# A mixed attention and MLP kernel: its written-out job order replaced by another, with the first four input tiles at the head of the DMA queue

## The chip, the cores and the metric

The kernel runs on one core of one Trainium2 chip. The time is device microseconds of one launch; lower is better. Three runs of the kernel before were timed: 707.80, 707.37 and 707.33 us, median 707.37 us. One further execution was taken by the hardware profiler; all rows quoted below come from it.

## The reference

For 2048 tokens of width 512 the reference computes `x + attention(xn) + mlp(xn)` with `xn = layernorm(x)`.

```
xn = layernorm(x)
# attention: 32 heads of width 16, the tokens in 4 segments of 512
q, k, v = xn @ wq, xn @ wk, xn @ wv
for s in range(4):                       # segments, in order
    a_dot = softmax(qs @ ks.T * scale + causal mask) @ vs
    a_mem = phi(qs) @ M / (phi(qs) @ z + 1e-6)
    o = g * a_mem + (1 - g) * a_dot
    M += phi(ks).T @ vs;  z += phi(ks).sum()
out_A = o @ wo
# mlp, per token
out_B = gelu(layernorm(xn) @ w1 + b1) @ w2 + b2        # 512 -> 1792 -> 512
return x + out_A + out_B
```

## The kernel before

**Number format.** Every large product is computed from float16 pairs: a value is split into a high and a low float16 half, and three products (high-high, high-low, low-high) are added in PSUM. The weights are scaled by powers of two that depend on their norms, so each weight must be loaded whole, squared and summed (`w_square`, ScalarE), turned into a scale (`w_scale`, a few tiny TensorE products and small ops), and split (`w_split`) before it can be used.

**Units.** The attention is cut into 16 units `i` (segment `i // 4`, group `i % 4` of 8 heads). A unit goes through these jobs:

- `T` or `T2`: the projections to queries and keys (TensorE, lines 497 or 528); the result is split into high and low halves, written to DRAM (`kd`, `qd`) and read back in another layout (`kst`, `qst`), all by the SP queue (lines 567 to 569 and 577).
- `M` (12 per unit): logits in PSUM (line 684) of which VectorE takes row maxima into `mc` (line 691). `R`: the maxima are transposed, written to DRAM (`md`) and read back as two more rows of `qst` (lines 704 and 707).
- `S` (12 per unit): logits again, transposed (line 724), then the exponential on ScalarE (line 729) into `pt` and the causal select on GpSimd (line 738).
- `pv`, `PV` (two times four): `pt` times values (line 753); `O` (three parts): division by the softmax sum; `Z`, `Qd`, `Q`: the memory part; `N`, `K`: the update of the memory.

**MLP.** It is cut into 16 half steps `j`: `D`/`D2` (products with w1, lines 497 and 528), `G` (seven Gelus on ScalarE with two table loads, lines 844 and 975), `H` (the split of the hidden values: GpSimd, ScalarE, GpSimd, lines 851 to 853), `e` (14 jobs of six products with w2, line 878). `V`/`V2` make values, `o2`/`out` the output projection, `X`/`Xt` the normalised input (loads at line 461, statistics at 407 to 422, transposes at 483 and 516), `ratio` a row of factors, `A` the accumulator loads.

**The loads.** `wl` issues weight loads on the SP queue: `qk` (the first column block of wk and wq, line 269), `QK` (the other three), `v`, `1a`/`1b` (the halves of w1, line 294), `2a`/`2b` (w2, line 297), `o`. `hold` is one small VectorE memset on the second block of wk. `wm` is `w_square`, `wf` is `w_scale`, `ws` is `w_split`.

**Fillers.** `warm` (14 jobs, line 922) are eight products of a tile of ones each whose result nobody reads.

**The order.** `streams()` makes lists of jobs; each list keeps its own order. The string `ORDER` merges them: each letter names a list, and the next job of that list is issued. The letters that matter here are: a input, c weight loads, C to J the preparation of the weight parts qk, QK, v, 1a, 2a, 1b, 2b, o, e constants, f and g the first segment's keys and queries, i `M` and `R`, j `S`, k `pv`, l `O`, m memory, n `V`, o `D`, p `G` and `H`, q `e`, r `out`, s `A`, t `warm`, u to z and A, B the paired jobs (`T2`, `V2`, `o2`, `D2`) in two phases. Since every engine takes its instructions in the order in which they are issued, this string is the order of TensorE, VectorE, ScalarE, GpSimd and of the SP queue's DMA issues alike.

```
bank = iter("".join(BANKS))
def dense():
    return dps.tile([P, 512], F32, name="ps" + next(bank), bufs=1)
...
todo = [iter(st) for st in streams()]
for c in "".join(ORDER):
    key = next(todo[NAMES.index(c)])
```

`BANKS` gives, for each PSUM tile that is asked for, which of the eight banks it takes. A job whose bank still holds a result that VectorE or ScalarE has not read yet waits on TensorE, and everything behind it.

Of the kernel before, what the change touches and what calls it, by code (L numbers as in the profile page):

```python
# [56 lines left out]
def streams():  # L57
# [59 lines left out]


ORDER = (
    "ecCcaacccCcaDDaaccDcDtCttttatDcaDctaatcCCtEeeDtEcbdfEtFFFDFGcFGFFgcEFEGFhDFoGfoFsoooEoiGotiDHcHGGHiicHcGEgHiGGE"  # L120
    "pHnIpniinioHiitiiHIDpHnIDIomciiooHhiqiqiqqDpjpqijqjqsijjioIijkHkHkkijsmIijqiqjqjiasqjjaIIfooIIipkkkkgplhAqpBAql"
    "jjBAljjqBpqijiqjqqiisIpkkkIkmiqjqiqijiqjqjqiqjjsfgsiiqqAJiqBJpikkkktaplphAlABBijApsijBjjijiqijqaaqippqqiqiqalak"
    "kmkkiqaqjqqjiqaqjqbaAjiBippmuijjvkkkkjApAjpBjlBlqhqjqqjqijqqiilkakkkjiqqJijqiqJqjjiqqjAiijBikpkkkJiiulwJJiJlmvl"
    "xymjjzwjjjxiAjikpskkkppiiBiyiijzjiqsjqjqjiqsiqjikmkkkphlqimulimvqAqjBjqlqjqjqjqjAammkkkkqjBijAjismjBjiAjiiBippk"
    "kkklAhipslBuimipvqqqqqqpiaqAqiqqiqqlmqiqBiApiBjApijiBijAjiBspjjiiaapkakkkmijijqjqhajajqqsiiqjqaakpmkkksillubmvq"
    "jqqqjqjqjqjAjqklkmkkmmjjBAjjiBjiwjikiikkpklxiiulhimlivAyBpqqiizipppqwiiqixiiqijqjqjjqjiqiqjiiskmkkksjiqqijqjqjA"
    "jisjBiypmhkkkkmpjpszjjllujmjvAAjBpmkkmlkkApBjBqqjqiqiqjqiqijqqjjiqqiqiaipmskkkpkhqqAiiBqipplqqsiupqliqmvqqsmlAj"
    "qqBjAqjqaAqBqqBiAiAspiappBijBAijjBaakaikkpkpiqijqjqiqjjqqqajjiqqqiipakkkkmiqaqaplqbqmlujmjvpAjjBjAhjBlkmkkkmjqp"
    "AjmiBjqijqqpjiqijqikkkklqiluimvwixiqiiqqqliqAiqqBpiiyjiijjzjjwijixiipksmkkksmjjyijjijzijspkkkkliAluimvqBpmqAqjB"
    "jAjqjmBpjqjqqiislkkkkiqjiqijqjqijiqjiqjqiikkppkklpAiilBuimvAqBpljqqjqjjqpAjqjBmkkkkiqjiqjqiqjjiqjqijqqiAsiBsipi"  # L130
    "ppkkikikpAAslpAiBilsBBqmqqqpqjplqqjqjqjqqjqjmkkpmkkjqqjqjjqqjjkkppkklllqqqqqqqqqqqrrrr"
)

BANKS = (
    "012345670234571265073241563702415637024156307241567302461730524612730546172305461732054732054270354270325743074"
    "250753402754302730542730542730574327430253026517425612574612547612457621462517642517642517651304276153042763105"
    "371640251367245024675024675024675204657206547123067123540623540635715274016534016534160534163045136401536145023"
    "767650231476502310231654371650271650247310247103246571247615023402736470326740327406320632327342067342067306175"  # L140
    "342107642710654327154327106543651027651027431043104365271065423765432714036510342765314027653102476351026351026"
    "365310265310261021602160251630164703164275167452031674013640137640512640512643705370512371237123075172513072512"
    "350172350172315701253706142671042536742536714025314530202671425367014730673140617430614370614376102576104376107"
    "610410341764103257641254103245176521470635214063756340765340765340765340765340762153765321453201475601473265010"
    "615302631053216302516302630251026531026531654702316503126035124607350746351027463510265310625317254063176317402"
    "540217521754021754021547012501427501472501245763012453012763012415276415276527641257641526741572461547263015264"
    "730156473232013256473256473256473256041736041736"
)


# [854 lines left out]
```

## Time and profile before

| | |
|---|---|
| median of three timed runs | 707.37 us (707.33 to 707.80) |
| the profiled execution's own time | 702.23 us |
| its span, first to last instruction | 700.5 us |
| TensorE busy | 681.1 us (97%), 8111 products |
| VectorE busy | 535.3 us (76%) |
| ScalarE busy | 522.9 us (75%) |
| GpSimd busy | 349.8 us (50%) |
| mean granted TensorE clock | 0.995 |

The span leaves out 1.7 us of the profiled execution around it. The timed runs are about 5.1 us longer than the profiled one. Rows of the profile name the engine (PE is TensorE, PEld its weight load, DVE VectorE, ACT ScalarE, POOL GpSimd, SPq the SP queue's issues), the line of the kernel, the operation and the tiles, written tile first. A busy TensorE is not a TensorE at its peak: the ends of products are modelled and overlap, so the time from one job's first product to the next job's is the better measure.

### The profile page before, as it was taken

The numbers are of one execution on the slowest core, as the hardware profiler recorded it, in microseconds if no ns is written. First come the engines' busy times: TensorE is split into PE (matmuls) and PEld (weight loads), VectorE is DVE, ScalarE is ACT, GpSimd is POOL, SyncE is SP. The second block draws the span as 40 slices with busy tenths as digits, with TensorE's granted clock in tenths as the row PEclk, the third lists the DMA queues.
The fourth block names the chain that finished last, engine by engine and source line by source line (L and its number), as shares of the span: only waits on it lengthen the run. The fifth ranks groups of instructions, "written<-read, shape, count | busy, mean of one in ns | idle before, by whom it ended". The sixth has DMA issues, their size and how long they took to land.

```text
span 700.5 us, 20441 instructions
## 1 busy us (share of the span) xinstructions
PE 681.1 (97%) x8111; PEld 421.1 (60%) x8111; DVE 535.3 (76%) x1695; ACT 522.9 (75%) x1013; POOL 349.8 (50%) x533
## 2 busy tenths in 40 slices
PE   8799999999999999999999999999999999999997
PEld 6464566575554577575566656577664656556533
DVE  4499877788588678899688847979778786969542
ACT  6989897778777668768883896677983667877970
POOL 5376667364524435646425355546462155464652
PEclk9899999999999999999999999999999999999999
DMA  9965222330402224022404224132031223131101
GB/s 283 264 188 185 65 62 63 76 78 18 124 3 82 67 72 104 29 68 62 107 3 122 46 50 137 17 109 47 5 92 47 78 76 94 17 103 37 19 1 60
DMA packets 51803, 55.33 MB, mean 79 GB/s; under 512 B 4782, under 2 KB 40636, under 8 KB 51708
## 3 DMA queue, kind: packets, MB, share of 16 engines
q1 hardware_dynamic: 49404, 49.84, 24.5%
q0 software_dynamic: 2304, 4.20, 3.6%
q8 instruction: 63, 1.03, 0.6%
q14 instruction: 32, 0.26, 0.1%
HBM read 36.99 MB, written 17.04 MB: 77 GB/s over the span
## 4 chain that ended last, share of the span: by engine, by line
PE 53%; ACT 15%; DMA 11%; DVE 9%; POOL 6%; issue 4%; SPq 2%; DVEq 0%; ACTq 0%; POOLq 0%
PE ps L528 20%; PE ps L878 12%; PE ps L753 8%; ACT pt L729 7%; PE ps L684 4%; DMA qd<-hl 3%; PE ps L724 3%; DMA qst<-qd 3%; DVE ps L691 2%; PE ps L497 2%; ACT hT L852 2%; PE ps L896 1%; ACT hT L844 1%; DVE hl L566 1%; POOL hT L853 1%
## 5 line engine op out<-in xcount | busy, mean ns | idle before, releaser
L691 DVE CUSTOM_DVE_ANT_0 ps<-ps,mask 128x512 f32<-128x512 f32 (+3 forms) x512 | 235.1, 521 | 26.2 <-PE ps L684 21.1
L729 ACT ACTIVATE pt<-ps,qkcs 128x512 f32<-128x512 f32 (+1 forms) x384 | 206.1, 627 | 30.3 <-PE ps L724 25.6
L878 PE MATMUL ps<-w2s,hT 64*128 64x512 f16 x1344 | 180.4, 376 | 0.6 <-ACT nD L762 0.3
L738 POOL TENSOR_SCALAR_AFFINE_SELECT pt<-pt 128x256 f32<-128x256 f32 x256 | 100.4, 424 | 104.0 <-ACT pt L729 103.3
L528 PE MATMUL ps<-xnT,w1s 64*128 64x256 f16 x2352 | 147.4, 269 | 0.4 <-ACT pt L729 0.3
L528 PEld LDWEIGHTS <-w1s 64*128 64x128 f16 x2352 | 121.8, 94 | 19.3 <-issue 1.6
L878 PEld LDWEIGHTS <-hT 64*128 64x128 f16 x1344 | 78.9, 94 | 52.2 <-issue 3.9
L853 POOL TENSOR_TENSOR hT<-hh,hT 128x512 f16<-128x512 f32 x64 | 67.1, 1049 | 76.9 <-ACT hT L852 76.9
L724 PE MATMUL ps<-qst,kst 50*128 50x256 f16 (+3 forms) x512 | 81.2, 296 | 2.6 <-DMA qst<-md 0.8
L684 PE MATMUL ps<-kst,qst 48*128 48x512 f16 (+3 forms) x512 | 77.8, 297 | 3.0 <-DVE mc L691 1.0
L753 PE MATMUL ps<-pt,vt 128*32 128x512 f32 (+3 forms) x1024 | 79.4, 436 | 0.5 <-POOL pt L738 0.5
L691 DVE DVE_READ_ACCUMULATOR2_ANT mc<- 128x1 f32 x512 | 71.2, 139 | 0.1
L528 PE MATMUL ps<-xnT,wqs 64*128 64x512 f16 x288 | 66.0, 376 | 0.0
L528 PE MATMUL ps<-xnT,wks 64*128 64x512 f16 x288 | 66.0, 376 | 0.0
L852 ACT ACTIVATE hT<-hh 128x512 f16<-128x512 f32 x64 | 36.8, 575 | 34.5 <-POOL hh L851 34.4
L825 DVE SCALAR_TENSOR_TENSOR hT<-ps,sc,sr 128x256 f32<-128x256 f32 x112 | 48.9, 476 | 14.1 <-PE ps L528 11.7
L753 PEld LDWEIGHTS ps<-pt,vt 128*32 128x32 f32 x1024 | 32.1, 109 | 42.0 <-issue 28.6
L851 POOL TENSOR_SCALAR hh<-hT,sc 128x512 f32<-128x512 f32 x64 | 42.4, 662 | 18.5 <-ACT hT L844 16.4
L684 PEld LDWEIGHTS <-qst 48*128 48x128 f16 x512 | 31.7, 94 | 28.8 <-issue 11.6
L724 PEld LDWEIGHTS <-kst 50*128 50x128 f16 x512 | 34.4, 94 | 24.0 <-issue 8.6
L844 ACT ACTIVATE hT<-hT,b1t 128x256 f32<-128x256 f32 x112 | 46.9, 496 | 1.7 <-DVE hT L825 1.5
L783 POOL TENSOR_TENSOR nN<-nN,oT 128x512 f32<-128x512 f32 x16 | 20.3, 1268 | 43.3 <-DVE oT L597 43.3
(227 smaller groups left out, 1021.5 us busy)
## 6 DMA issues: line engine op xcount, KB each, us to landing
kd<-hl SPq DMA_DIRECT2D x48, 128.0 KB
kst<-kd SPq DMA_DIRECT2D x32, 192.0 KB
qd<-hl SPq DMA_DIRECT2D x48, 128.0 KB
qst<-qd SPq DMA_DIRECT2D x32, 192.0 KB
acc<-in_A_x_dram SPq DMA_DIRECT2D x16, 256.0 KB
acc<-in_B_b_dram POOLq DMA_DIRECT2D x16, 256.0 KB, 4.0
out_dram<-acc SPq DMA_DIRECT2D x16, 256.0 KB
xt<-in_A_x_dram SPq DMA_DIRECT2D x14, 256.0 KB
```

The lines of the kernel that those rows point to most:

```text
L528: w = T.matmul(ps[a], lhs(a, k, u)[r], rhs(a, k, v)[r], start=ph == 0 and k == 0 and m == 0, stop=ph == 1 and k == n - 1 and m == 2, skip_ ...
L684: T.matmul(p[:, o:o + n], stk[i, 0][r, t, P * qb:P * qb + P], stk[i, 1][r, t, :n], start=True, stop=True)
L691: V.tensor_tensor_reduce(p[:, o:o + n], p[:, o:o + n], mask[:, 512 - n:], 1.0, -3e38, OP.add, OP.max, mc[:, 16 * b + 4 * t + qb:16 * b + 4 ...
L724: T.matmul(p[:, o:o + n], stk[i, 1][r, t, P * kb:P * kb + P], stk[i, 0][r, t, P * kb:], start=True, stop=True)
L729: A.activation(e[:, OFF[kbs[0]]:OFF[kbs[0]] + o], p[:, :o], AF.Exp, scale=qkcs[:, 1, i % NG:i % NG + 1])
L738: G.affine_select(v, v, pattern=[[0, 2], [1, P]], compare_op=OP.is_ge, fill=0.0, base=0, channel_multiplier=-1)
L753: T.matmul(p[32 * c:32 * c + 32, P * kb:], vt[s, kb][:, 4 * g + c, 16 * odd:16 * odd + 32], pt[i, 2 * c + odd][:, OFF[kb]:OFF[kb] + LEN[kb ...
L825: V.scalar_tensor_tensor(hzs[fh][:, fi, :], p[:, :256], col(F1 + fh), srow[hs][:, 256 * hh:256 * hh + 256], op0=OP.mult, op1=OP.mult)
L844: A.activation(z, z, AF.Gelu_apprx_tanh, bias=b1t[:, FH * (j % 2) + f:FH * (j % 2) + f + 1])
L852: A.activation(hT[:, z, 0, :], t, AF.Copy)
L853: G.tensor_tensor(hT[:, z, 1, :], t, hT[:, z, 0, :], op=OP.subtract)
L878: w = T.matmul(pes[j][a], hTs[fh][r, fi, u, P * a:P * a + P], w2s[r, fo, v, :], start=n == 0 and m == 0, stop=fi == FH - 1 and m == 2, ski ...
```

## The change

`ORDER` and `BANKS` are replaced by other strings of the same length (1307 letters, 1158 digits). Each letter occurs as often as before, so the same jobs are issued and each list keeps its own order; what changes is how the lists are merged, and which bank each PSUM tile takes.

```diff
 ORDER = (
-    "ecCcaacccCcaDDaaccDcDtCttttatDcaDctaatcCCtEeeDtEcbdfEtFFFDFGcFGFFgcEFEGFhDFoGfoFsoooEoiGotiDHcHGGHiicHcGEgHiGGE"
-    "pHnIpniinioHiitiiHIDpHnIDIomciiooHhiqiqiqqDpjpqijqjqsijjioIijkHkHkkijsmIijqiqjqjiasqjjaIIfooIIipkkkkgplhAqpBAql"
...
-    "ppkkikikpAAslpAiBilsBBqmqqqpqjplqqjqjqjqqjqjmkkpmkkjqqjqjjqqjjkkppkklllqqqqqqqqqqqrrrr"
+    "eettaccaCtCcDDcactCaDacDCcDDceccttttaatacaCDEtEbDttccDfdFFFDaFEGFFccEGFsgEDFoGFEFgchFEfoooHoGHGiGHHiioGGsoHppnc"
+    "iiiniiGGniiHHIHniiHooDImiqhiqiipIooiIDpqjqpscijqqjijiqiHIjqqijEHqiIImkkkkoIsjiqjsojjiqHjjafIoiIqkkpkkgplApqABIj"
...
+    "sspppkkkplsAiiBABiABqqppplqqjjqjljmqjqjqmqpmkkkkqqjqjqjqjqjqqjppkkkkqqqqqqqqlqqlqqlrrrr"
 )
 BANKS = (
-    "012345670234571265073241563702415637024156307241567302461730524612730546172305461732054732054270354270325743074"
+    "012345670123567403142573610425731642057316424057316402576314025763140257631402631402631402630124603126402631460"
...
```

Read out, the SP queue's issues begin, before, with wk and wq block 0, then the four tiles of the first 512 tokens, then `QK` (three), `v` (two), the two small loads, `1a`, `2a`. After, they begin with two input tiles, wk and wq block 0, the other two input tiles, then `QK`, `v`, the small loads, `1a`, `2a` as before; the loads `X(1,0,0)` of the next segment follow the first projection's write-out, where before they came some 130 jobs later. The fillers stand, before, at places 21 to 53, 89, 125 and 289 of the order; after, at places 2 to 50, 349 and 602 (twelve of them ahead of the first projection, against ten before). In both, the first projection `T(0,0,1)` is followed on TensorE by the scale of `1a` before the second projection `T(0,0,0)`; before, the scale of `v` and a filler stand between the two as well.

More of the change, by code (lines that the diff above doesn't have):

```diff
@@ L119 @@
 ORDER = (
-    "ecCcaacccCcaDDaaccDcDtCttttatDcaDctaatcCCtEeeDtEcbdfEtFFFDFGcFGFFgcEFEGFhDFoGfoFsoooEoiGotiDHcHGGHiicHcGEgHiGGE"
-    "pHnIpniinioHiitiiHIDpHnIDIomciiooHhiqiqiqqDpjpqijqjqsijjioIijkHkHkkijsmIijqiqjqjiasqjjaIIfooIIipkkkkgplhAqpBAql"
-    "jjBAljjqBpqijiqjqqiisIpkkkIkmiqjqiqijiqjqjqiqjjsfgsiiqqAJiqBJpikkkktaplphAlABBijApsijBjjijiqijqaaqippqqiqiqalak"
-    "kmkkiqaqjqqjiqaqjqbaAjiBippmuijjvkkkkjApAjpBjlBlqhqjqqjqijqqiilkakkkjiqqJijqiqJqjjiqqjAiijBikpkkkJiiulwJJiJlmvl"
-    "xymjjzwjjjxiAjikpskkkppiiBiyiijzjiqsjqjqjiqsiqjikmkkkphlqimulimvqAqjBjqlqjqjqjqjAammkkkkqjBijAjismjBjiAjiiBippk"
@@ L125 @@
[L125 to L129, printed above, removed]
@@ L130 @@
-    "jAjqjmBpjqjqqiislkkkkiqjiqijqjqijiqjiqjqiikkppkklpAiilBuimvAqBpljqqjqjjqpAjqjBmkkkkiqjiqjqiqjjiqjqijqqiAsiBsipi"
-    "ppkkikikpAAslpAiBilsBBqmqqqpqjplqqjqjqjqqjqjmkkpmkkjqqjqjjqqjjkkppkklllqqqqqqqqqqqrrrr"
+    "eettaccaCtCcDDcactCaDacDCcDDceccttttaatacaCDEtEbDttccDfdFFFDaFEGFFccEGFsgEDFoGFEFgchFEfoooHoGHGiGHHiioGGsoHppnc"
+    "iiiniiGGniiHHIHniiHooDImiqhiqiipIooiIDpqjqpscijqqjijiqiHIjqqijEHqiIImkkkkoIsjiqjsojjiqHjjafIoiIqkkpkkgplApqABIj"
+    "pAjlBjjBjqhpqqjilkikJkkiIaiqqjiqjqjjqiqjiqqijcfgqiiqAiqiBkkkpkipAlmJpBAlhiBijApjiBisjqjqijqaqaqpsjqiiqialiqpsak"
@@ new lines @@
+    "kkkmpaqqqjqiqjqitjaAabBiJpjuijjvJkkkmkpjAqjqqjplqBjAqlBjjqqiiqilJkkkkiqijqjqiqjiqjjqAiaJhjBiiJkkkkplAiuiBiJmvwj"
+    "mjxlwjjjlaxyiijzipsikpkkkpiiyjjizjjqqijqiqijqismkkkkplimshlqquimvqqqjAalqjBjjqqjjqAmkkkkjsiBjAjijBiAjjiBiismkkp"
+    "mpkklspilAuhBimipvqpqiqqqqqAqiqiqqmqqiqBiiAiBpitplijApijBjjiAjijBaskiapkkkimajjqqhqaijajqjqqjiaakikkkplmqlsbumj"
+    "vjqqqjqqjqjAjlqmkkkkjBjmjihimjAijiBjiikkkkpilipwiulimvplmAxpyiiBziwiisxiiqqijpqjqiqijqjqjiqiqqjikkkkmsasjiqjqqi"
+    "jqjAihjBjypkkkkmjpzjjsllumjjvAApBjBlpmkkkmkAqBjpqmqjiqiqjqqjiqijqiqjppsAiiqqiBhqqipkkkklqppqqiiuiqlsqimvqqAjqqq"
@@ L132 @@
+    "qqjajBqAlmABqBiAiApapiBjBpjiAiijBasakkkpkpaiqijqqjiqijjqjqqajpiqqiskkkkamqiaqapqqlhbqumljjmjvAjpAjBjlBkkkmkjAjj"
+    "BjmijqiqqjiqipipkkkklmuiliqqmqvqiqqwiqiixiqqiqAiiBilpyjijzijpwjjjxiiskipmskkkjjyijmsjijzjikkkkpliquqlimvAqmlqjB"
+    "AjBjAjqmjBjqisipkkkksiqijqijqjqjiqijqijqiqpipkkkklpAiiBluimvAqBpljqqjqjqjApjqjBmkkkkqijqijqqjiqjijqiqjqiAiBiiki"
+    "sspppkkkplsAiiBABiABqqppplqqjjqjljmqjqjqmqpmkkkkqqjqjqjqjqjqqjppkkkkqqqqqqqqlqlqqlrrrr"
 )
 BANKS = (
-    "012345670234571265073241563702415637024156307241567302461730524612730546172305461732054732054270354270325743074"
@@ L138 @@
[L138 to L147, printed above, removed]
+    "012345670123567403142573610425731642057316424057316402576314025763140257631402631402631402630124603126402631460"
@@ new lines @@
+    "321406321640321362401362401362574062406214305672305762057632057623057360253765302765302531402765312405312756340"
+    "763517264107421607412607412607410276347516302476023514670514670542632632170632170632170631273106237106237150465"
+    "074162350741354162354135074162074162354351620743516207417642013756471536453716453716471647157315764315726405674"
+    "321054302156743145637021456370237140237145637563756021437561450234576513746052173452317460521746035217465246521"
+    "476154276152746161746174561274120374516325071463205762305761243057612437643760152015243760143760512431205142310"
@@ new lines @@
+    "452310452310453214053210457362457362140562174305630567472413056724156742174567241576254715471546271305461305130"
+    "513134613460513274605270513274601535346012753461026134601263041263041263041263047512637512675306740617245306145"
+    "732046517326513726513751375126372637263571260471263504325604756132756132705461273054670354637504162375047504203"
+    "475342750275032475032754023702543750423570354270163540163270163563427563427342756347254763245762345736240157243"
+    "601574321574603215743215743215743215743261057261"
```

## The prediction

> **What bounds the kernel now.** First the page's totals, then who TensorE waits for, then single stretches.
>
> ```profile
> span 700.5 us, 20441 instructions
> ...
> PE 681.1 (97%) x8111; PEld 421.1 (60%) x8111; DVE 535.3 (76%) x1695; ACT 522.9 (75%) x1013; POOL 349.8 (50%) x533
> ```
>
> TensorE has work for all but 19.4 us. The order neither removes nor adds a product, so it can gain only from those 19.4 us, from slow products, and from ends that the busy time covers. In the view of waits (time, times, longest) the named part is small:
>
> ```profile
> PE ps L360 <- ACT w1s L328: 3.8, 2, 2.6
> ...
> PE ps L684 <- DVE mc L691: 1.0, 2, 0.8
> PE ps L684 <- DMA qst<-qd: 0.9, 2, 0.5
> ```
>
> The largest is the start. In the timeline (start, length, idle time before):
>
> ```profile
> 0.82 0.44 SPq L269 DMA_DIRECT2D wks<-in_A_wk_dram  x1
> ...
> 1.86 0.97 SPq L461 DMA_DIRECT2D xt<-in_A_x_dram  x2
> ...
> 5.74 0.69 DVE L407 BATCH_NORM_STATS2 st<-xt 128x6 f32<-128x512 f32 x1 [4.76 <-DMA xt<-in_A_x_dram]
> ...
> 11.50 5.52 SPq L294 DMA_DIRECT2D w1s<-in_B_w_dram  x4
> ...
> 18.68 2.76 PE L497 MATMUL ps<-xnT,wks 128*128 128x512 f16 x12
> ...
> 23.45 1.70 ACT L328 ACTIVATE w1s<-w1s 128x1792 bf16<-128x1792 f32 x1 [0.40 <-DMA w1s<-in_B_w_dram]
> ...
> 27.11 0.59 PE L360 MATMUL ps<-am,ones 128*128 128x1 f32 x2 [1.23 <-ACT w1s L328]
> ...
> 27.98 4.36 PE L497 MATMUL ps<-xnT,wqs 128*128 128x512 f16 x12
> ```
>
> The reader sees three clocks of the start. The input tiles let VectorE begin at 5.74 us; the first projection `T(0,0,1)` runs at 18.68; the second, `T(0,0,0)`, stands behind the scale of w1's first half, which waits for w1 to land (23.4 us) and for ScalarE's squares, until 27.1. The table by stretches (length, busy time of each engine, granted clock) shows the rest:
>
> ```profile
> 24.00:25.00 1.00, 0.00 (x0) 0.00 (x0) 0.72 (x3) 1.00 (x1) 0.00 (x0) 0.72 1.05 389
> ...
> 30.00:31.00 1.00, 1.00 (x4) 0.38 (x3) 0.00 (x0) 1.00 (x4) 0.07 (x1) 0.50 0.21 70
> 31.00:32.00 1.00, 1.00 (x6) 0.40 (x5) 0.00 (x0) 1.00 (x1) 1.00 (x1) 0.86 0.00 0
> ...
> 60.00:70.00 10.00, 9.19 (x97) 5.23 (x94) 8.47 (x32) 9.14 (x17) 7.02 (x9) 1.00 0.37 93
> ...
> 650.00:660.00 10.00, 9.97 (x133) 6.09 (x133) 7.94 (x21) 9.87 (x18) 6.35 (x7) 1.00 0.10 19
> 660.00:670.00 10.00, 9.91 (x91) 4.41 (x88) 2.46 (x4) 9.89 (x19) 7.10 (x12) 1.00 0.08 15
> ```
>
> From 24.4 us (clock 0.72 as a mean of one stretch) to 31.3 us the granted clock is 0.50, so the twelve products of `T(0,0,0)` take 4.36 us where the same twelve took 2.76 at 18.68. From 28 to 650 us TensorE is nearly full. From 650 to 676 us ScalarE is the full engine.
>
> **The change part by part.**
>
> *The head of the DMA queue.* Ahead of w1's first half both orders load the same: 0.5 MB of first blocks, 1 MB of input, 1.5 MB of `QK`, 1 MB of `v`, 1.8 MB of w1. Two input tiles pass 0.5 MB of weights; the other two stay behind the same 1 MB of neighbours. VectorE can begin on the first two perhaps 2 us sooner, but the joint statistics need all four tiles, which end at the same byte. `T(0,0,1)` gains about 1 us (an estimate: two of four 0.69 us statistics done early). That gain then meets the wait at 23.45 us: w1 lands behind the same bytes, ScalarE squares it for the same 3.6 us, TensorE still has the scale of `1a` ahead of `T(0,0,0)`. So both kernels stand at about 28 us with the same projections done. Value 0. Bounds: the best is that the half clock is gone when `T(0,0,0)` begins, 4.36 − 2.76 = −1.6; the worst that it lasts for a second stretch of 6.9 us (24.4 to 31.3), in which a full TensorE does half its work, +3.4. The input tiles `X(1,0,0)` now pass two parts of `1b` in the queue; `1b`'s scale keeps its place in the order (job 106 in both), with more `D` and `T` products ahead of it: 0.
>
> *The fillers.* Of 14, eleven stood before 28 us, and three behind, where TensorE has other work:
>
> ```profile
> 45.49 1.04 PE L922 MATMUL ps<-ones 128*128 128x256 f16 x8
> ...
> 61.89 0.99 PE L684 MATMUL ps<-kst,qst 48*128 48x256 f16 x4
> 62.99 1.03 PE L922 MATMUL ps<-ones 128*128 128x256 f16 x8
> 63.96 0.50 PE L684 MATMUL ps<-kst,qst 48*128 48x384 f16 x6
> 64.87 1.46 PE L497 MATMUL ps<-wvs,xnT 128*128 128x512 f16 x6 [0.41 <-DVE mc L691]
> ```
>
> After, two stand behind 28 us. One filler less is −1.0 (bounds: 0, if a wait takes its place, and −1.0).
>
> *The first unit's maxima.* The same fence shows a cluster: from 61.89 to 62.99 four products of `M` take 1.10 us, and from 63.96 to 64.87 six take 0.91, where VectorE is the late one. At full pace the pairs take about 0.43 each time (a pair of 512 columns side by side is 0.22). That is 1.1 us lost. After, `V(0,1)`, `V(0,2)` and `V(0,3)`, each 2.6 us of TensorE work (half of it is the 1.46 row), stand between the pairs `M 3 to 5`, `6, 7`, `8, 9`, `10, 11`. Value −1.1; bounds 0 (VectorE had other work here, 8.47 of 10 us) and −1.1.
>
> *The round trip from projection to first maxima.* `M(i,0)` needs `kst` and `qst`, which go through DRAM. I counted the TensorE work that the order puts between a unit's projection and its `M(i,0)`, with these rows: a job `e` is 0.65 us (two in 1.46 with the end), a pair of `D2` phases 2.6, the four `pv` 2.4.
>
> ```profile
> 660.96 1.46 PE L878 MATMUL ps<-w2s,hT 64*128 64x512 f16 x12
> ...
> 517.16 1.47 PE L528 MATMUL ps<-xnT,w1s 64*128 64x256 f16 x24
> ...
> 192.77 2.36 PE L753 MATMUL ps<-pt,vt 128*32 128x512 f32 x32
> ```
>
> Before, from unit 2 on, three units have 12.1 us or less (2, 4 and 12), and the view of waits gives 0.9 us to this cause. After, six have (2, 6, 8, 12, 13, 14, the least 11.4: unit 8 lost an `e`, a `D2` phase and two `S` from its cover). Three more at 0.9 / 3 is +0.9. Bounds: 0 (a filled bank hides it) and +1.5 (0.5 each, the longest).
>
> *Clusters of `M` and `S`.* Each hands TensorE's bank to VectorE or ScalarE for longer than it took to fill:
>
> ```profile
> L691 DVE CUSTOM_DVE_ANT_0 ps<-ps,mask 128x512 f32<-128x512 f32 x128 | 86.9, 717 | 13.9 <-PE ps L684 13.0 <-PE ps L724 0.4
> ...
> 552.01 0.52 PE L724 MATMUL ps<-qst,kst 50*128 50x512 f16 x2
> 552.23 0.41 PE L684 MATMUL ps<-kst,qst 48*128 48x256 f16 x2
> 552.85 0.62 PE L684 MATMUL ps<-kst,qst 48*128 48x512 f16 x2 [0.20 <-DVE mc L691]
> 553.28 0.87 PE L724 MATMUL ps<-qst,kst 50*128 50x384 f16 x6
> ```
>
> Here five in a row hold TensorE from 552.01 to 553.97, 2.0 us for about 0.9 us of products: 1.1 lost. Over the trace I find a loss of 0.04 us for a lone `M` or `S`, 0.18 for two in a row, 0.22 for three, 0.77 for four and five. Before there are 140, 80, 19 and 6 such rows, after 131, 95, 18 and 2: 28.1 us against 27.9 us. Value −0.2. Bounds ±3: −3 if the four long rows that go take their loss with them, +3 if the fifteen new pairs cost as much as the dearest do.
>
> *The end.* ScalarE is full here, in one chain:
>
> ```profile
> 654.13 3.04 ACT L844 ACTIVATE hT<-hT,b1t 128x256 f32<-128x256 f32 x7
> ...
> 670.02 6.20 ACT L729 ACTIVATE pt<-ps,qkcs 128x512 f32<-128x512 f32 x12
> ...
> 677.41 0.63 ACT L852 ACTIVATE hT<-hh 128x512 f16<-128x512 f32 x1 [1.19 <-POOL hh L851]
> ```
>
> The last Gelus need the last `D2`; behind them both orders have 28 jobs `e`, unit 15's `S`, `pv` and `O`, and four `out`, and between the last Gelus and the last exponential ScalarE has the same jobs. The new order spreads `e` more evenly among the `S`; that moves TensorE's waits, not ScalarE's end. ScalarE is idle for 0.24 us from 650 to 670. Value −0.2; bounds −0.3 and +0.7 (one `e` too late).
>
> *Sum.* 0 − 1.0 − 1.1 + 0.9 − 0.2 − 0.2 = −1.6 us: span 698.9, the profiled execution's own 702.23 us becomes 700.6, and the median of the runs, which lies 5.1 us higher and moves with it, 707.37 − 1.6 = **705.8 us**, 0.23% faster.
>
> One rule of the Trainium skill bears on the start (TensorE: Matmul & The Clock Gate, Part 1: The HAM clock gate): the clock goes to half after a free-running window of about 3.4 us without work and comes back after one busy window. The trace agrees as far as it goes: 0.50 from 24.4 us, back at 31.3, 3.3 us into `T(0,0,0)`. The new order has no product between `T(0,0,1)`, its small transpose and the `1a` scale, so by the rule the half clock comes for certain, but leaves 3.4 us after 28 us at the latest, 1.7 us lost against the 1.6 lost now. By the page, rival C below would need a further idle window and is less likely than I make it.
>
> **The rivals.**
>
> A, the forecast: small gains near 60 us, a little back in round trips: 705.8 us. For it: each term has a row. Against it: four of five terms are near the size of a single wait.
>
> B, the middle gets tighter than counting shows. Rows of two and more `M` and `S` cost 23 us (28.1 less 140 × 0.04). If the new banks and neighbours take a quarter, it is −5.8 more: 700.0 us. For it: 0.04 against 0.18 us shows how much a neighbour matters. Against it: there are as many such rows as before, 245 and 246, and VectorE and ScalarE have the same work.
>
> C, slower: the half clock lasts for a second stretch, to about 38 us. Place: between `T(0,0,1)` and the `1a` scale, where the filler and the scale of `v` no longer stand. It decides if TensorE, after 28 us, has to wait again for the splits of w1 (ScalarE is full there, 1.00 at 30 us), so that the clock isn't given back. Price +3.4: 705.8 + 3.4 = 709.2 us. Against it: at 30 us TensorE is busy 1.00 even now.
>
> D, nothing: the waits only change places. w1's landing holds the start and ScalarE the end, and what is saved near 60 us is lost at the next `M`: 707.2 us.
>
> **How the numbers follow.** A difference of 0.2%, 1.4 us, is about what a measurement of this kernel can tell from none. Chances: A 0.40, B 0.25, C 0.18, D 0.17. A's own range is 703.5 to 707; just over half of it lies beyond 1.4 us. Faster: 0.24 of A, all of B and 0.01 of D, 0.50. Same: 0.15 of A and 0.13 of D, 0.28. Slower: 0.18 of C, 0.01 of A and 0.03 of D, 0.22. The range takes B with it and reaches past C: 699.5 to 710.
>
> **What would show it.** Right: w1's squares begin at 23 to 24 us and `T(0,0,0)` at 27.5 to 28.5; two fillers behind 28 us; 60 to 70 us with TensorE over 9.7 of 10; three to six round-trip waits of 0.3 to 0.5 us; from the last Gelus to the end within 0.7 us of now (46.4 us from 654.1). Wrong: `T(0,0,0)` ahead of 26 us, which would mean that w1 landed early and the queue's head mattered; a stretch at half clock behind 32 us (C); busy time of TensorE moving by over 3 us between 100 and 650 us (B, or its reverse).

## The result and the profile after

Timed against the kernel before, the changed kernel is faster: a median of 699.12 us against 705.31, ratio 0.992 with an interval of 0.9896 to 0.9943. In a second, later timing it was 698.12 against 703.91, ratio 0.9928 (0.9902 to 0.9955). So the change brings 5 to 6 us. The forecast was 1.6 us. Its sign was right, its size was not.

The profiled execution took 698.73 us, 3.5 us less than the 702.23 of before.

First the page of after, the lines that answer to those of before:

```profile
span 697.0 us, 20435 instructions
...
PE 677.4 (97%) x8111; PEld 432.8 (62%) x8111; DVE 533.4 (77%) x1695; ACT 523.4 (75%) x1013; POOL 351.2 (50%) x533
```

The products are the same 8111. TensorE's busy time is 3.7 us shorter and its idle time the same (19.6 us against 19.4). Its waits (time, times, longest), though, are not fewer:

```profile
PE ps L360 <- ACT w1s L328: 5.0, 2, 3.6
PE ps L684 <- DMA qst<-qd: 2.7, 7, 0.6
PE ps L724 <- ACT pt L729: 1.8, 4, 0.8
...
PE ps L483 <- POOL xt L430: 1.3, 1, 1.3
```

The wait at the start went from 3.8 to 5.0 us, that for the projection's round trip from 0.9 to 2.7. All the waits that the view lists came to 13.1 us and come to 14.2. By these rows alone one would expect a slower kernel. The timeline of the start, after:

```profile
19.16 2.75 PE L497 MATMUL ps<-xnT,wks 128*128 128x512 f16 x12
...
23.80 1.70 ACT L328 ACTIVATE w1s<-w1s 128x1792 bf16<-128x1792 f32 x1 [0.17 <-DMA w1s<-in_B_w_dram]
...
27.46 0.59 PE L360 MATMUL ps<-am,ones 128*128 128x1 f32 x2 [1.44 <-ACT w1s L328]
...
28.34 0.99 PE L360 MATMUL ps<-am,ones 128*128 128x1 f32 x4
29.19 5.17 PE L497 MATMUL ps<-xnT,wqs 128*128 128x512 f16 x12
```

`T(0,0,0)` begins 1.2 us later than before and takes 0.8 us longer. The scale of `v` (line 360, x4) now stands just ahead of it, at half clock, and takes 0.99 us. (The section on the change names it between the two projections for the kernel before alone; it stands there in both, but behind the scale of `1a` now.) Before, it stood in an idle place:

```profile
21.28 0.50 PE L360 MATMUL ps<-am,ones 128*128 128x1 f32 x4
```

The table by stretches (length, busy PE, PEld, DVE, ACT, POOL, then the granted clock, DMA share and GB/s):

```profile
27.00:28.00 1.00, 0.54 (x3) 0.54 (x3) 0.00 (x0) 0.97 (x5) 0.00 (x0) 0.65 1.17 298
...
33.00:34.00 1.00, 1.00 (x4) 0.44 (x3) 1.00 (x2) 1.00 (x2) 1.00 (x2) 0.50 1.05 283
34.00:35.00 1.00, 1.00 (x10) 0.72 (x8) 0.95 (x1) 1.00 (x3) 0.41 (x1) 0.94 1.16 183
...
60.00:70.00 10.00, 10.00 (x111) 5.64 (x111) 9.82 (x39) 7.51 (x17) 7.41 (x8) 1.00 0.39 97
```

The half clock now lasts from 27.3 us (0.65 as the mean of that stretch) to 34.1 (0.94), where before it lasted from 24.4 to 31.3. In the second profile of the changed kernel, which comes below, it lasts from 24.7 to 35.0. At 60 to 70 us TensorE is full, where it had 9.19 of 10. The maxima of the first unit now have values (`V`) between them:

```profile
61.34 0.50 PE L684 MATMUL ps<-kst,qst 48*128 48x256 f16 x4
61.77 2.76 PE L497 MATMUL ps<-wvs,xnT 128*128 128x512 f16 x12
64.47 0.50 PE L684 MATMUL ps<-kst,qst 48*128 48x384 f16 x6
```

The four products have 0.43 us until the next job begins, and so have the six (to 64.90 us), where they had 1.10 and 0.91 before. And the end, from the last Gelus:

```profile
650.76 2.90 ACT L844 ACTIVATE hT<-hT,b1t 128x256 f32<-128x256 f32 x7
```

From 650.76 to the span's end at 697.0 are 46.2 us; before it was 46.4.

**A curve that finds the place.** The order of jobs differs, so rows can't be set side by side. I gave each TensorE job the median of its kind's time in the trace of before, and read off when each kernel has done the same amount of that work. Fillers count as no work, so one that is taken out shows as a gain. Each column is in us, against the first profile of the kernel before, whose time stands at the left; the kernels are described below.

| time in before | after | after, 2nd | before, 2nd | `abb` | `baa` | `aba` | `rt_cover` | `best` |
|---|---|---|---|---|---|---|---|---|
| 30 | +1.6 | +1.5 | +0.8 | +1.3 | +1.1 | +1.2 | +2.3 | +2.3 |
| 56 | +1.3 | +1.3 | +1.3 | +3.7 | +0.9 | +1.3 | +2.2 | +3.1 |
| 65 | −1.4 | −1.4 | +0.8 | +1.0 | +0.9 | −1.4 | −0.5 | +0.4 |
| 87 | −2.1 | −2.2 | +0.7 | +0.3 | +0.9 | −2.1 | −1.3 | +0.3 |
| 215 | −4.1 | −4.4 | +2.4 | −1.1 | +1.6 | −4.1 | −3.4 | −2.0 |
| 255 | −4.1 | −4.6 | +2.5 | −1.0 | +1.5 | −3.9 | −3.4 | −1.8 |
| 360 | 0.0 | −0.4 | +2.4 | +0.1 | +5.4 | −2.8 | +5.8 | −1.9 |
| 402 | −1.9 | −2.3 | +2.5 | +0.1 | +3.9 | −2.8 | +3.8 | −1.8 |
| 567 | −2.8 | −3.6 | +3.9 | −0.7 | +2.6 | −3.9 | +3.0 | −2.6 |
| end | −3.5 | −4.1 | +4.0 | −0.7 | +2.0 | −4.5 | +3.0 | −3.2 |

Before's fillers behind 28 us stand at 45.5, 63.0 and 140.4 us, after's at 164.2 and 306.3. The reader should see three things: a gain of 3.4 us from 56 to 87 us, another of 2.0 to 215 us, and a loss of 4.1 us from 255 to 360 us (1.0 of it a filler), of which about half comes back at once.

### The profile page after: what moved, and what is told of

It reads as the page before. It is cut to its first block, busy times and chain, and to the rows that moved or that the text cites. A ratio compares the mean times of both kernels' runs of the same rounds, so it can differ in the third digit from the quotient of the medians.

```text
span 697.0 us, 20435 instructions
## 1 busy us (share of the span) xinstructions
PE 677.4 (97%) x8111; PEld 432.8 (62%) x8111; DVE 533.4 (77%) x1695; ACT 523.4 (75%) x1013; POOL 351.2 (50%) x533
## 4 chain that ended last, share of the span: by engine, by line
PE 63%; ACT 13%; DMA 10%; DVE 6%; POOL 4%; issue 3%; SPq 1%; ACTq 0%; DVEq 0%; POOLq 0%
PE ps L528 25%; PE ps L878 14%; PE ps L753 7%; PE ps L684 5%; ACT pt L729 4%; DMA qd<-hl 4%; DMA qst<-qd 4%; PE ps L497 3%; PE ps L724 3%; DVE ps L691 2%; ACT hT L844 2%; PE ps L896 2%; POOL hT L853 1%; ACT hT L852 1%; DMA w1s<-in_B_w_dram 1%
## 5 line engine op out<-in xcount | busy, mean ns | idle before, releaser
L729 ACT ACTIVATE pt<-ps,qkcs 128x512 f32<-128x512 f32 (+1 forms) x384 | 206.9, 626 | 31.3 <-PE ps L724 24.8
L878 PEld LDWEIGHTS <-hT 64*128 64x128 f16 x1344 | 82.0, 94 | 49.1 <-issue 5.7
L724 PE MATMUL ps<-qst,kst 50*128 50x512 f16 (+3 forms) x512 | 79.1, 297 | 3.0 <-ACT pt L729 1.8
L684 PE MATMUL ps<-kst,qst 48*128 48x256 f16 (+3 forms) x512 | 77.8, 297 | 3.9 <-DMA qst<-qd 2.7
L753 PE MATMUL ps<-pt,vt 128*32 128x512 f32 (+3 forms) x1024 | 77.9, 436 | 0.0
L753 PEld LDWEIGHTS ps<-pt,vt 128*32 128x32 f32 x1024 | 30.5, 109 | 42.9 <-issue 30.5
L684 PEld LDWEIGHTS <-qst 48*128 48x128 f16 x512 | 34.5, 94 | 27.8 <-issue 10.0
L628 DVE TENSOR_SCALAR ame<-ps,bg 64x512 f32<-64x512 f32 x24 | 18.0, 750 | 31.3 <-POOL nN L785 19.5
```

Of the source, the lines that this page charges most:

```text
L684: T.matmul(p[:, o:o + n], stk[i, 0][r, t, P * qb:P * qb + P], stk[i, 1][r, t, :n], start=True, stop=True)
L724: T.matmul(p[:, o:o + n], stk[i, 1][r, t, P * kb:P * kb + P], stk[i, 0][r, t, P * kb:], start=True, stop=True)
L729: A.activation(e[:, OFF[kbs[0]]:OFF[kbs[0]] + o], p[:, :o], AF.Exp, scale=qkcs[:, 1, i % NG:i % NG + 1])
L753: T.matmul(p[32 * c:32 * c + 32, P * kb:], vt[s, kb][:, 4 * g + c, 16 * odd:16 * odd + 32], pt[i, 2 * c + odd][:, OFF[kb]:OFF[kb] + LEN[kb ...
L878: w = T.matmul(pes[j][a], hTs[fh][r, fi, u, P * a:P * a + P], w2s[r, fo, v, :], start=n == 0 and m == 0, stop=fi == FH - 1 and m == 2, ski ...
```

## The experiments

**Does the head of the queue do anything? (`loads_head`, `front_new`, `rest_new`)** `loads_head` is the order before with only the first loads moved. The other two are halves, cut at `M(0,7)`: the changed order up to there and the order before behind it, and the reverse.

```diff
 loads_head, the first line of ORDER
-    "ecCcaacccCcaDDaacc...
+    "eaccaCcccCcaDDaacc...
 front_new
-  order before, all jobs
+  changed order to M(0,7); order before for the rest
 rest_new
-  order before, all jobs
+  order before to M(0,7); changed order for the rest
```

> The order before, with its first letters alone changed so that two input tiles, the first blocks of wk and wq, and the other two input tiles lead the SP queue, as in the order after; all else and all banks as before. Theory 'place' (the gain lies in the stretches from about 55 us on, not in the queue's head): w1's squares still begin at 23 to 24 us, the second projection still at 27.5 to 28.5 us, time within 1.4 us of before. Rival 'queue' (the loads at the head are the gain): the second projection over 1.5 us earlier, time 3 us or more below before.

Measured: ratio 1.0005 (0.9981 to 1.0028). The queue's head alone brings nothing that can be measured, as the forecast's 0 had it. The start came later than expected, w1's squares at 24.46 us and `T(0,0,0)` at 28.71; but the second profile of the kernel before, which comes below, has 24.53 and 28.77, so this need not be the loads' doing.

> The new order up to M(0,7), then all that is left in the order before (banks taken along). Theory 'place': the start of the new order costs 1.3 to 1.8 us (longer wait for the 1a scale, half clock in the second projection), the rest is as before: span 0.5 to 2.5 us longer than before. Rival 'queue': 3 us or more shorter, since the new start is all in it.

> The order before up to M(0,7), then all that is left in the new order. Theory 'place': keeps the old start, about 1.3 us better than the new one, and has the new order's gains behind it, less the fillers (two of them behind 28 us, plus the one at 45 us in the old start): span 3.5 to 5.5 us below before, 0 to 2 us below after. Rival 'queue': within 1.4 us of before.

Measured: `front_new` 1.0026 (0.9996 to 1.0057), `rest_new` 0.9964 (0.9947 to 0.9982). `rest_new` was to be 3.5 to 5.5 us faster and is 2.2 to 2.5. The two halves don't add up to the whole, and the curve points to why: the cut lies in the middle of the 56 to 65 us where the whole wins 2.7 us. `rest_new` wins 0.8 there; `front_new` loses 2.3, and its profile has a stretch at half clock from 66.0 to 69.4 us, behind two waits for w1's splits. So these halves don't tell how much of the gain lies behind the start; a cut must be put where nothing is in flight.

**The fillers in the start's gap (`fill_gap`).** Four fillers of the changed order are moved to stand behind `par2`, ahead of w1's squares, where TensorE waits.

```diff
 ORDER, by jobs
-  warm 10, warm 11 ahead of T(0,0,1); warm 12, warm 13 later
+  T(0,0,1), par2, warm 10, warm 11, warm 12, warm 13, wm 1a
```

> The new order with four of its fillers moved: the two ahead of the first projection and the two among the later work now stand between the first projection's small transpose and the 1a scale, where TensorE was idle from 21.9 to 25.6 us. Theory 'clock': with 1.5 us as the longest idle stretch there, no half clock; the second projection takes 2.8 us in place of 5.2 (-2.4) and two fillers no longer stand among the later work (-2.0): 4.4 us below after, 692 to 694 us of span. Rival 'the fillers count, the clock does not': half clock as before, only -1 to -2 against after. Second rival: the two later fillers had filled waits, then only the -2.4.

Measured: ratio 0.9937 (0.9912 to 0.9962), as the whole change and not 4.4 us better: all three expectations failed. The half clock at the start did not go; it was one stretch of 3.4 us instead of two, and the start 0.8 us earlier than after's. And two new stretches of 3.4 us came, at 49.8 us, behind a wait of 2.32 us for `qst`, and at 353.6 us. More of this kind below.

**Which stretch makes the difference? (`abb`, `baa`, `aba`)** The order is now cut where both have issued nearly the same jobs: behind `PV(3,1)`, about 208 us in the trace of before (a filler, a Gelu job and three splits of wo differ), and behind `PV(8,1)`, about 410 us (one input load differs).

```diff
 abb
+  changed order to PV(3,1); order before for the rest
 baa
+  order before to PV(3,1); changed order for the rest
 aba
+  changed order to PV(3,1); order before to PV(8,1); changed order for the rest
```

> The changed order up to the job PV(3,1) (about 211 us), the order before from there on (the last filler stands where the changed order has it, so none is taken out). Theory (stretch by stretch): the gain made up to 211 us, 4.1 us by the profiles, of which 2 to 3 us come from fillers put later, is kept but for the last filler's 1.0 us, since the rest is the old order: 3 us faster than the kernel before. Rival (the gain lies in the GpSimd wait at line 861, near 470 us): this kernel keeps that wait, so it stands within 1 us of the kernel before. Rival (phases): waits ahead of M and S fall elsewhere once the lead differs, and the lead drifts by over 2 us behind 211 us in either direction.

> The order before up to PV(3,1), the changed order from there on. Theory (stretch by stretch): no gain up to 211 us; from 215 to 360 us the changed order loses about 3 us beside its later filler, from 360 us to the end it wins 3.5 us, and the GpSimd wait at line 861 is gone, another 1 to 2 us: 1 to 2.5 us faster than the kernel before. Rival (the GpSimd wait alone): 5 us faster, as the whole change.

> The changed order up to PV(3,1), the order before from there to PV(8,1) (about 400 us), the changed order from there to the end. Theory (stretch by stretch): the changed order loses about 2 us net between 215 and 400 us, so putting the old order there keeps the lead of 4 us and adds the later gains: 1.5 to 2.5 us faster than the whole change, 7 us faster than the kernel before. Rival (phases): what the changed order loses there is what it had won by being early (both meet the same late engine at 360 us), so the middle doesn't matter and this kernel is within 0.7 us of the whole change.

Measured on one chip: `abb` 0.9976 (0.9957 to 0.9995), `baa` 0.9997 (0.9979 to 1.0015), `aba` 0.9926 (0.991 to 0.9942).

Read with the curve, the parts hold their place. In `baa` the changed order loses 3.9 us from 255 to 360 us (in after 3.1 beside its filler) and wins 3.4 us from there to the end (in after 3.5). In `aba` the middle of before costs 1.1 us from 255 to 360 us, a filler's worth. So these differences belong to the order and not to what ran ahead of it: the phase rival for the drift falls. Order and banks were always moved together, though; what the banks alone are worth was not tried. Three expectations failed in size. `abb` was to be 3 us faster and is 1.9 by the medians; its profile has a further stretch at half clock at 50.1 us. `baa` was to be 1 to 2.5 us faster and isn't, although the wait at line 861 of the next experiment is gone from it; `aba` was to beat the whole change by 1.5 to 2.5 us, and its median of 698.68 us stands within 0.6 us of both medians of the whole change. In the profiles it is ahead by 1.0 and 0.4 us, less than the timing can tell.

**The queue behind an accumulator load (`a11_early`).** In the trace of before, on the SP queue and on GpSimd:

```profile
466.17 0.79 SPq L577 DMA_DIRECT2D qst<-qd  x2
467.01 0.44 SPq L857 DMA_DIRECT2D acc<-in_A_x_dram  x1
```

```profile
471.27 0.90 POOL L861 DMA_DIRECT2D acc<-in_B_b_dram  x1 [2.44 <-issue]
471.93 1.80 POOL L430 TENSOR_SCALAR xt<-xt,stats 128x512 f32<-128x512 f32 x2
```

The load `A(11,0)` (line 857) can't be issued before the read-back of `qst`, which waits for its own data. The accumulate on GpSimd (line 861) then waits for the load, and line 430 and all of GpSimd behind it. The experiment moves the load ahead of eleven jobs.

```diff
 ORDER, by jobs
-  A(10,1), M(10,11), T2(11,0), ..., T2(11,1), e(9,5), e(9,6), A(11,0)
+  A(10,1), A(11,0), M(10,11), T2(11,0), ..., T2(11,1), e(9,5), e(9,6)
```

> One job of the order before is moved: the accumulator load A(11,0), which stood behind the second projection T2(11,1) of unit 11, now stands 12 jobs earlier, behind A(10,1). Theory (the queue): on the SP queue that load stood behind the read-backs of kst and qst, so GpSimd's accumulate A(11,1) found its tile not yet landed and the whole GpSimd queue waited up to 4 to 6 us for it, holding X(3,0,2) and H(10,0) behind it; that costs 1 to 2 us in a usual execution of the kernel before. Then the longest wait at line 861 falls from 4.1 us to under 0.1 us and the time by 1 to 2 us against the kernel before. Rival (covered): TensorE has other work in that place, the wait goes and the time stays within 0.5 us.

The group of line 861 (times in ns: shortest, median, longest), before and in the experiment:

```profile
L861 POOLq EVENT_SEMAPHORE  x11: 17/43/4129, 244.7 to 656.0; - x11
```

```profile
L861 POOLq EVENT_SEMAPHORE  x11: 17/43/43, 245.8 to 656.4; - x11
```

The wait is gone, and the time is 0.999 (0.9973 to 1.0006): 0.7 us less by the medians, no difference that can be told, and less than the 1 to 2 us of the theory. The changed order has no such wait either (43 ns at most). So it accounts for at most 1.9 us of the gain, by the interval's end.

**Was the first profile of before a usual one? (`before_again`, `after_again`)** Both kernels unchanged.

> The kernel before, unchanged, profiled once more and timed against itself. Theory (a lucky first profile): the first profiled execution of the kernel before, 702.23 us, had its start 0.6 to 1.1 us earlier than the three other kernels that begin with the same order, and paid nothing on TensorE for the GpSimd wait at line 861; a second one is 703 to 705 us, with T(0,0,0) 0.5 to 1.5 us later. The ratio is 1.000 within its interval. Rival (usual): it is within 0.5 us of 702.2, and the gap between the profiles' difference (3.5 us) and the timed one (5.6 us) stays unexplained.

> The changed kernel, unchanged, profiled once more and timed on the same chip as the two kernels below. Theory (places, not chance): the stretches of the curve repeat: a gain of 2.7 us between 56 and 65 us, about 2 us between 87 and 215 us, a loss of 4 us (filler included) between 255 and 360 us, regained by 1.9 us to 402 us; timed 5 us faster than the kernel before (4 to 6). Rival (half clock by chance): a stretch at half clock falls between 40 and 70 us, as in two of the eight kernels with new parts, and the profile is 2 to 3 us longer than 698.7.

Measured: `before_again` has ratio 0.9993 (0.9973 to 1.0013), as it must, and its profiled execution took 706.19 us, 4.0 us more than the first and above the 703 to 705 expected; `T(0,0,0)` began at 28.77 us, 0.8 later. The first profile lies 1.7 us below the median of 703.91, the second 2.3 above. `after_again`'s took 698.12 us, 0.6 us less than the first, and its column of the curve repeats the first's stretch by stretch. Taken as means the pairs stand at 704.2 and 698.4 us, 5.8 us apart, close to the timed difference. The waits of the second profile of before tell where most of its 4 us are:

```profile
PE ps L684 <- DMA qst<-qd: 2.9, 5, 0.8
...
PE ps L724 <- DMA qst<-md: 1.9, 2, 1.3
```

and its timeline from 112 to 185 us:

```profile
116.07 0.39 PE L684 MATMUL ps<-kst,qst 48*128 48x512 f16 x1 [0.78 <-DMA qst<-qd]
...
149.60 0.81 PE L724 MATMUL ps<-qst,kst 50*128 50x512 f16 x2 [1.30 <-DMA qst<-md]
182.25 0.66 PE L724 MATMUL ps<-qst,kst 50*128 50x512 f16 x2 [0.60 <-DMA qst<-md]
```

Round trips through DRAM cost it 4.8 us, against 1.7 in the first profile. Two kinds must be kept apart. The maxima's trip (`qst<-md`, from `R` to `S(i,0,0)`) holds TensorE for 0.8 to 1.9 us between 40 and 215 us in all six profiles that have the units from 1 on in the order before there (before, `before_again`, `a11_early`, `baa`, `loads_head`, `front_new`; mean 1.2), and in none of the eight that have them in the changed order. Both trips together are 2.4 us as a mean of the six and 1.1 of the eight. So 1.3 us of the gain is this, on average. By the curve's means the pairs are 2.9 us apart between 87 and 215 us (−2.1 against +0.9), so it is less than half of that; the rest was not taken apart.

What the maxima's trip waits for is seen on the SP queue. Before:

```profile
130.12 2.75 PE L497 MATMUL ps<-xnT,wqs 128*128 128x512 f16 x12
...
141.53 0.80 SPq L577 DMA_DIRECT2D qst<-qd  x2
142.38 0.43 SPq L857 DMA_DIRECT2D acc<-in_A_x_dram  x1
142.91 0.38 SPq L704 DMA_DIRECT2D md<-mhl  x1
...
146.30 0.53 SPq L707 DMA_DIRECT2D qst<-md  x2
```

and after:

```profile
128.32 2.75 PE L497 MATMUL ps<-xnT,wqs 128*128 128x512 f16 x12
...
139.01 0.80 SPq L577 DMA_DIRECT2D qst<-qd  x2
140.53 0.30 SPq L704 DMA_DIRECT2D md<-mhl  x1
...
143.87 0.53 SPq L707 DMA_DIRECT2D qst<-md  x2
144.45 0.36 SPq L857 DMA_DIRECT2D acc<-in_A_x_dram  x1
```

In both, the maxima of unit 2 are written (line 704) behind the read-back of unit 3's `qst` (line 577), which waits for its own data. Before, only the issue of the accumulator load (line 857) lies between the two, so the end of the trip hangs on the projection `T(3,0)` and not on `R(2)`. After, 0.7 us pass between them, and the trace names VectorE's last step on the maxima (line 702) as what the write waits for. From that projection's end to the read-back of the maxima are 13.4 us before (132.87 to 146.30) and 12.8 after (131.07 to 143.87). The difference lies ahead of line 577, which is issued 8.7 us after the projection's end before and 7.9 after; from there on it is 4.8 us before and 4.9 after. So in this pair it isn't the load's place (0.5 us) that takes the wait away.

Nor is it more cover: TensorE's own work from the projection's end to `S(2,0,0)`, its wait left out, is 14.4 us in each of the six profiles, and in the changed order it can be as little as 14.2. It is the trip that is shorter, 13.8 us as a mean of the six and 12.7 of the eight. Why the projection's own read-back comes earlier was not tried.

**More cover for the round trip (`rt_cover`).** In the changed kernel the largest waits of this kind are at `M(8,0)`:

```profile
348.94 0.39 PE L684 MATMUL ps<-kst,qst 48*128 48x512 f16 x1 [0.23 <-DMA qst<-qd]
349.97 0.39 PE L684 MATMUL ps<-kst,qst 48*128 48x512 f16 x1 [0.65 <-DMA qst<-qd]
...
351.20 1.05 PE L528 MATMUL ps<-xnT,w1s 64*128 64x256 f16 x16 [0.16 <-DVE mc L691]
```

```diff
 changed ORDER, by jobs (one PSUM tile had to take another bank)
-  S(7,1,2), M(8,0), N(8), M(8,1), Z(8), S(7,3,0), D2(4,1,0)
+  S(7,1,2), D2(4,1,0), M(8,0), N(8), M(8,1), Z(8), S(7,3,0)
-  M(14,0), A(13,1), M(14,1), H(12,3), pv(13,0,0)
+  pv(13,0,0), M(14,0), A(13,1), M(14,1), H(12,3)
```

> The changed order with two first maxima put behind one more job of TensorE: D2(4,1,0) ahead of M(8,0), pv(13,0,0) ahead of M(14,0). Theory (round trip): in the changed kernel M(8,0) waits 0.23 and 0.65 us and M(14,0) 0.44 us for kst and qst; the moved jobs are as long as these waits, so 0.8 to 1.3 us are won against the changed kernel, most of it near 350 us. Rival (the wait only changes its place): VectorE's maxima come late there, so the next M waits for its bank instead; within 0.4 us of the changed kernel.

Measured: ratio 1.0006 (0.9988 to 1.0023), so the whole gain is lost; neither expectation had this. TensorE at the place:

```profile
348.81 0.27 PE L528 MATMUL ps<-xnT,w1s 64*128 64x256 f16 x1
350.70 1.90 PE L528 MATMUL ps<-xnT,w1s 64*128 64x256 f16 x23 [1.62 <-ACT pt L729]
352.22 0.81 PE L684 MATMUL ps<-kst,qst 48*128 48x512 f16 x2
354.35 0.69 PE L516 MATMUL ps<-ident,phk 64*128 64x64 f32 x8 [1.32 <-DVE mc L691]
...
357.05 0.61 PE L724 MATMUL ps<-qst,kst 50*128 50x384 f16 x4 [0.90 <-DVE mc L691]
```

`M(8,0)` waits for its data no more. But the moved `D2(4,1,0)` keeps its bank, and there, that much earlier, an exponential still holds it: it waits 1.62 us, and two waits for VectorE follow. Then the clock falls:

```profile
351.00:352.00 1.00, 1.00 (x19) 0.95 (x17) 0.00 (x0) 0.00 (x0) 0.17 (x1) 0.80 0.00 0
352.00:353.00 1.00, 1.00 (x7) 0.30 (x3) 0.11 (x1) 0.00 (x0) 0.00 (x0) 0.50 0.00 0
...
361.00:362.00 1.00, 1.00 (x10) 0.36 (x10) 1.00 (x5) 0.98 (x3) 0.59 (x2) 0.58 0.00 0
```

From 351.6 (0.80 as the mean of that stretch) to 361.8 us (0.58) it is 0.50. The mean clock of its 12 timed executions is 0.989 as a median, that of the changed kernel's 21 is 0.993, so such stretches are hardly an accident of one profile. In the curve this kernel stands at −3.4 at 255 us, as after, and at +5.8 at 360 us, where after is at 0.0. The lever itself stays open: the move needs another bank. What is shown is the price of the bank: 5 us by the curve, 6 by the medians (704.44 against 698.12), of which only the first 1.6 is the wait.

**Together (`best`).** `aba` with its last two fillers moved into the start's gap.

```diff
 aba, by jobs
-  warm 12 at about 164 us, warm 13 at about 306 us
+  T(0,0,1), par2, warm 12, warm 13, wm 1a
```

> The changed order to PV(3,1), the order before to PV(8,1), the changed order to the end, and the last two fillers moved ahead of w1's squares, where TensorE has an idle gap. Theory: 1.0 us (the middle, by the two profiles) and 2.0 us (two fillers of 1.04 us off the full part) faster than the changed kernel: 695 to 697 us. Rival (the fillers are free): TensorE's later stretches are held by VectorE and ScalarE, and the two fillers' time goes into waits: 697.5 to 699 us.

Measured: ratio 0.9918 (0.9898 to 0.9939), median 698.71 us against the changed kernel's 698.12 on the same chip. It doesn't beat it, and the 695 to 697 us expected were not reached. Between 87 and 215 us `best` moves by −2.3 and `aba`, with its filler at 164 us, by −2.0: that filler was nearly free. From 255 to 360 us `best` stays and `aba` loses 1.1: the filler at 306 us did cost its 1.04 us. The 1.8 to 2.4 us by which `best` is behind `aba` from 65 to 255 us were there at 56 us already: its start is 1.1 us late at 30 us and 1.8 at 56. The two fillers in the gap did not keep the clock up: it was 0.50 from 28.5 to 35.3 us, and `T(0,0,0)` took 5.28 us.

## Why the prediction was right, and where it was not

Point by point, by the forecast's terms.

*The head of the queue, 0.* As a lever it was right (`loads_head`, 1.0005). w1's squares at 23.80 us were inside the 23 to 24 that I gave. `T(0,0,0)` at 29.19 us was not inside 27.5 to 28.5. The step that failed: "both kernels stand at about 28 us with the same projections done". They don't: the scale of `v` had been named as one that moves away from ahead of the `1a` scale, and its new place, between that scale and `T(0,0,0)`, was not priced. It is 0.99 us at half clock. The half clock was to leave "3.4 us after 28 us at the latest"; it left at 34.1 us, and at 35.0 in the second profile. So "1.7 us lost against the 1.6 lost now" failed as well: the twelve products took 5.17 us, 2.4 more than at full clock. The trace also agrees less than the forecast says with its rule for the clock: before, the clock fell at 24.4 us, 1.8 us after the last product of a filler (22.7 us), not after a stretch of 3.4 us without work. And `T(0,0,1)` did not gain its 1 us (19.16 us against 18.68). The start cost 1.3 us at 56 us, with the filler at 45.5 us already taken out; against before's second profile, which has the same 1.3 there, nothing.

*The fillers, −1.0: right.* Each is 1.04 us where TensorE is full; three leave, two come. `best` shows the other bound at work: one of the two that came was nearly free.

*The first unit's maxima, −1.1: right in place, a little small.* Full TensorE at 60 to 70 us was foreseen as over 9.7. From 56 to 65 us the curve gives −2.7, of which 1.04 is the filler at 63 us: −1.7. The two clusters, 1.10 and 0.91 us before and 0.43 each after, are 1.15 of it.

*The round trip, +0.9: wrong.* The waits at line 684 rose by 1.8 in the first pair of profiles; the longest of them, at unit 8, was named. But in the second pair they fell from 2.9 to 1.3 us. Two things were missing. One is the second round trip of each unit, from `R` to `S(i,0,0)` through `md`: my step counted the cover of `M(i,0)` alone, although the page of before lists the wait `qst<-md`, 0.8 us, which is this trip; its wait is gone in the changed order, 1.2 us as a mean. The other is that waits of this kind differ between executions, 1.7 us against 4.8 in one kernel, so one profile is a poor price for them. What stands ahead of the maxima's write on the SP queue was not followed.

*Clusters, −0.2 (±3): inside its bounds.* The sum was not right: 28.1 us is the loss as found before, 27.9 is the rounded losses times the rows of after. Rounded losses on both sides give 28.8 against 27.8, −1.0. By the same count as in the forecast, rows of one, two, three and more `M` and `S` lose 6.0, 15.0, 3.8 and 1.2 us after, 26.0 against 28.1. The four long rows that went did take their loss with them. That is 2.1 us, about a third of the 5.8 that rival B needed, so B's 700.0, near the measured median, is near it by another way. (B's "245 and 246" rows count the lone ones too; of two and more there are 105 before and 115 after.)

*The middle as a whole: not seen.* From 87 us on the forecast had +0.9 − 0.2 − 0.2. The first profiles show −2.0 to 215 us, +4.1 to 360 us and −3.5 to the end. Part of the +4.1 is named: the filler 1.0, `M(8,0)` and what follows it 1.0 (0.23, 0.65 and 0.16), and a wait of 0.6 us for `phq` at 261.2 us. The other 1.5, and what wins 1.9 us from 360 to 402 us, were not taken apart.

*The end, −0.2: right, −0.1.* ScalarE holds it.

*The sum against the median.* The sum was laid on a profiled execution 5.1 us below the median of three runs, on the assumption that the median "moves with it". It doesn't, and the base was high: the 14 runs behind 705.31 include the three that gave 707.37, and the other eleven have a median of 703.85. The profiled execution, on the other hand, was one of the shorter ones, with few of the waits that the change removes. Before's second profile is 4.0 us longer than its first, 3.1 of it in round trips; after's second is 0.6 us shorter. So the pairs' means are 5.8 us apart, where the first profiles are 3.5 and the timings say 5 to 6. As a difference that is within the 7.9 us that the range allows; the median of 699.12 us itself lies 0.4 below its lower end of 699.5.

*Rival C* came in part. Its sign, half clock behind 32 us, is there: to 34.1 us, and to 35.0 in the second profile. Its 38 us and its price of 3.4 us are not: `T(0,0,0)` took 0.8 us longer. Further stretches at half clock, well behind the start, came in `abb`, `fill_gap`, `front_new`, `loads_head` and `rt_cover`, and in neither profile of the changed kernel.

## What to carry over

A profile is one execution: a wait for a DMA round trip that is 0.8 us in it may be 1.3 in the next, so price the waits by a second profile or by kernels that share the stretch, and don't assume that a median moves by what a profile shows. When an order is rearranged, follow every DMA past every trip on its queue: one that is issued behind a read-back that waits for its own data becomes a wait on another engine. And a job moved to cover a wait needs its PSUM bank free by then, or it makes a longer one.

## What was not expected of the hardware

Half clock comes in the middle of the run, far from the start, and a second execution of the same stretch may not have it. It comes in stretches of about 3.4 us (50.1 to 53.5 in `abb`, 117.6 to 121.0 in `loads_head`) or a multiple (6.8 at after's start, 10.2 in `rt_cover`). In `abb`, whose order is the changed one up to about 208 us, after these two waits:

```profile
47.59 0.39 PE L684 MATMUL ps<-kst,qst 48*128 48x512 f16 x1 [1.20 <-DMA qst<-qd]
48.49 0.71 PE L684 MATMUL ps<-kst,qst 48*128 48x512 f16 x7 [0.51 <-DMA qst<-qd]
```

the clock fell:

```profile
50.00:51.00 1.00, 1.00 (x7) 0.72 (x6) 1.00 (x4) 0.97 (x4) 0.68 (x1) 0.55 0.00 0
51.00:52.00 1.00, 1.00 (x7) 0.74 (x5) 1.00 (x5) 1.00 (x3) 1.00 (x2) 0.50 0.61 153
```

In after, with 0.49 us of waiting at the same place, it did not: `abb` is 2.4 us behind by 56 us. In `loads_head` two waits were enough:

```profile
115.24 0.39 PE L684 MATMUL ps<-kst,qst 48*128 48x512 f16 x1 [0.82 <-DMA qst<-qd]
116.26 0.39 PE L684 MATMUL ps<-kst,qst 48*128 48x512 f16 x1 [0.63 <-DMA qst<-qd]
```

```profile
117.00:118.00 1.00, 1.00 (x13) 0.49 (x10) 1.00 (x5) 1.00 (x2) 0.39 (x1) 0.80 0.00 0
118.00:119.00 1.00, 1.00 (x7) 0.74 (x5) 0.97 (x6) 1.00 (x4) 0.83 (x4) 0.50 0.00 0
```

The same pair in `before_again`, 0.42 and 0.78 us, and a single wait of 1.30 us there brought none. So 1.45 us in two pieces did and 1.30 in one did not; I give no threshold. The price, by an estimate from the clock of 0.50, is the wait and about 1.7 us more for each stretch, half of 3.4, if TensorE has work in it.

The Trainium skill (TensorE: Matmul & The Clock Gate, Part 1: The HAM clock gate) has the length of these stretches, with a window of about 3.4 us that runs by itself, and warns of idle gaps of that length. The length agrees. The gaps here were of 0.5 to 2.3 us, with products between them; the same page's section on a second HAM failure mode, psum-queue depth-cycling, speaks of micro-idles between groups of products, and that is nearer to what these traces show.
